# Four early pairs of q and k staged in the tile of w_in's sums, in a fused attention and feed-forward kernel, with every engine's order written anew

## The chip, the core and the metric

The kernel runs on one core of a Trainium2 chip. The metric is the device time of one execution in microseconds: three runs of the kernel before gave 353.08 as their median (352.15 to 353.31). The profile is a fourth execution; its own time was 353.37 us, and the span that its trace covers, from the first instruction to the last, is 351.6 us.

The engines are named as the profile names them: PE is TensorE (PEld its weight loads), DVE is VectorE, ACT is ScalarE, POOL is GpSimd and SP is SyncE. A `q` behind a name, as in SPq, is that engine's queue of DMA issues.

## The reference

Eight batches of eight-head attention with a bias that depends on the distance of two positions, then a feed-forward layer with a squared ReLU on all 4608 rows:

```python
scores = scale * np.matmul(q, k.transpose(0, 1, 3, 2))      # q, k, v: (8, 8, 576, 64)
scores = scores + bias.transpose(2, 0, 1)[None, :, :, :]    # bias_table[bucket(|i - j|)]
attn = softmax(scores)                                       # over the keys
x = np.matmul(attn, v).transpose(0, 2, 1, 3).reshape(4608, 512)
h = np.maximum(x @ w_in, 0.0)                                # w_in: (512, 2048)
out = (h * h) @ w_out                                        # w_out: (2048, 512)
```

Inputs and output are float32. The kernel computes in float16 with float32 sums.

## The kernel before

**Tiling.** Two heads make a pair, four pairs a batch, so there are 32 pairs, numbered from 0. A pair's q and k are loaded in natural layout into staging tiles (`qs`, `ks`, float16, 128x768), turned so that the head's 64 dimensions lie on partitions (`qt`, `kt`), and multiplied to scores in PSUM (line 954; the last 64 keys at line 1021 or 1149 through `kz`, which holds the two heads' keys on its diagonal; the last 64 queries at line 961). ScalarE takes the exponential into `pt` and `pm` (lines 976, 1006, 1030, 1136, 1159), VectorE multiplies by the exponential of the bias, kept in `tb_sb` (line 800), TensorE multiplies by v with a column of constants beside it that gives the row sums (`va` holds 4 tiles of 128 keys, `vm` the last 64 keys; lines 826 and 833, later 876 and 892), and VectorE divides by the row sums into `x`. x is turned into `xt`, and 512 rows at a time (a group, nine of them) go through the feed-forward layer. The first layer is line 1551 for group 0, plain, and line 1486 for the others, with seven products of sub-blocks in place of eight; the second layer is line 1331, with seven as well.

**Sums of weights.** The seven products need sums and differences of blocks of w_in. They lie in the tile `sw` (128 partitions, four parts of three blocks of 512 float16, so each part is 1536 wide); VectorE makes them in `late_sums` (line 1408), before group 1. Until then `sw` holds nothing.

**Staging.** There are three pairs of staging tiles, `qs`/`ks` 68/69, 70/71 and 72/73, handed out in turn to all 32 pairs by the ring `r_stg`. The load of pair p waits until pair p-3 has been turned. Pair 0 comes by two hardware queues in float32 (k from ACTq, q from SPq) into the tile `g` and is cast into its staging tile by ScalarE (line 650). Pairs 1 to 31, v of batches 0 and 1, and the weights are loaded by POOL with a cast on the way (line 428); at most eight of POOL's loads are under way at once (eight lanes, each with its own semaphore). In batches 0 and 1, TensorE turns q and k (line 1089) and VectorE or ScalarE copies them out of PSUM (lines 786 and 788); from batch 2 on, SP turns them by DMA.

**Batch 0 in halves.** For pairs 0 to 3 the queries are worked in two parts (256 and 320), so that group 0's first half can start after the first part of all four pairs: scores of three exponential steps per pair, then the values, then the transposition of x (line 1209), then group 0's first layer (line 1551).

**What sets the order.** Each step of the work is an operation with a number. The table `TURNS` gives for each engine the numbers in the order in which that engine is to issue them. `Plan.schedule` walks the five lists with a cost for every operation, to lay the five streams into one program and to choose buffers where a ring has several free. An engine issues strictly in its list's order, and waits at the head of its list for operands and buffers.

Of the kernel before, what the change touches and what calls it, by code (L numbers as in the profile page):

```python
# [40 lines left out]
LATE, T_STG = 7, 8  # L41
V_AFTER = 8
# [8 lines left out]
def _bucket(n):  # L51
# [42 lines left out]
""",  # L94
    "ACT": """
# [16 lines left out]
""",  # L112
    "DVE": """
# [214 lines left out]
def mm(n):  # L328
    return n / 2.4 + 2.5
# [6 lines left out]
def dve(n, rate=1.0, fix=160.0):  # L336
    return fix + n / (0.96 * rate)
# [1307 lines left out]
```

## Time and profile before

| | before |
|---|---|
| median of 3 runs | 353.08 us (352.15 to 353.31) |
| the profiled execution | 353.37 us |
| its span | 351.6 us |
| PE busy | 341.0 us, 97% |
| DVE busy | 311.4 us, 89% |
| ACT busy | 264.5 us, 75% |
| POOL busy | 164.4 us, 47% |

A busy PE is not PE at its peak: the ends of matmuls are modelled, and a stretch can be full of matmuls that run slowly. PEclk is the granted clock of TensorE (1.00 is full). The table by stretches gives each engine's busy time in a stretch, with the number of instructions in brackets. In the timeline a row is a run of like instructions: the start in us, the busy time in us, engine and line, the tile written and the tile read, their number, and in brackets the idle time of that engine just before the row and what ended it.

### The profile page before, as it was taken

The numbers are of one execution on the slowest core, as the hardware profiler recorded it, in microseconds if no ns is written. First come the engines' busy times: TensorE is split into PE (matmuls) and PEld (weight loads), VectorE is DVE, ScalarE is ACT, GpSimd is POOL, SyncE is SP. The second block draws the span as 40 slices with busy tenths as digits, with TensorE's granted clock in tenths as the row PEclk, the third lists the DMA queues.
The fourth block names the chain that finished last, engine by engine and source line by source line (L and its number), as shares of the span: only waits on it lengthen the run. The fifth ranks groups of instructions, "written<-read, shape, count | busy, mean of one in ns | idle before, by whom it ended". The sixth has DMA issues, their size and how long they took to land.

```text
span 351.6 us, 11335 instructions
## 1 busy us (share of the span) xinstructions
PE 341.0 (97%) x4672; PEld 278.0 (79%) x4672; DVE 311.4 (89%) x615; ACT 264.5 (75%) x370; POOL 164.4 (47%) x287
## 2 busy tenths in 40 slices
PE   8599999899999999999999999999999999999996
PEld 7378777777877887778877887787768988888885
DVE  4869999999998999799989998879998996899983
ACT  4879998499998689889978587869797952288300
POOL 6929587859787369684683495245100000000000
PEclk9989999999999999999999999999999999999999
DMA  9999999999999999999999999699622031200023
GB/s 164 134 201 185 187 152 164 177 135 137 133 158 175 218 134 135 152 191 162 164 69 161 185 113 157 130 162 122 88 69 81 2 59 54 67 32 3 30 84 126
DMA packets 161379, 44.39 MB, mean 126 GB/s; under 512 B 144688, under 2 KB 161328, under 8 KB 161328
## 3 DMA queue, kind: packets, MB, share of 16 engines
q0 software_dynamic: 74144, 14.53, 49.9%
q1 hardware_dynamic: 86928, 28.86, 45.9%
q8 instruction: 36, 0.59, 0.7%
q10 hardware_dynamic: 256, 0.30, 0.3%
q14 instruction: 15, 0.12, 0.1%
HBM read 36.94 MB, written 9.44 MB: 132 GB/s over the span
## 4 chain that ended last, share of the span: by engine, by line
PE 79%; DVE 9%; DMA 5%; ACT 4%; issue 1%; POOL 1%; SPq 0%; DVEq 0%; POOLq 0%
PE bank L1331 29%; PE bank L1486 25%; PE bank L892 8%; PE bank L954 7%; DVE g L1512 2%; DMA va<-in_v_dram 2%; DMA qt<-qs 2%; PE bank L833 2%; DVE pt L800 2%; ACT pt L1136 2%; PE bank L1551 2%; PE bank L1149 1%; DVE s L1290 1%; PE bank L961 1%; DVE g L447 1%; DVE x L915 1%
## 5 line engine op out<-in xcount | busy, mean ns | idle before, releaser
L1136 ACT ACTIVATE pt<-bank 128x1024 f16<-128x1024 f32 x112 | 110.2, 1035 | 14.5 <-PE bank L954 13.8
L428 POOL DMA_DIRECT2D qs<-in_q_dram x79 | 55.8, 710 | 28.8 <-DMA qt<-qs 17.4
L428 POOL DMA_DIRECT2D ks<-in_k_dram x79 | 55.6, 712 | 21.8 <-DMA kt<-ks 12.1
L800 DVE TENSOR_TENSOR pt<-pt,tb_sb 128x512 f16<-128x512 f16 (+3 forms) x108 | 61.1, 589 | 2.8 <-ACT pt L1136 1.7
L1331 PEld LDWEIGHTS <-g 128*128 128x128 f16 x576 | 54.5, 98 | 9.4 <-issue 2.2
L1512 DVE CUSTOM_DVE_ANT_0 g<-bank,y 128x512 f16<-128x512 f32 x88 | 58.5, 682 | 1.9 <-PE bank L1486 0.5
L1486 PEld LDWEIGHTS <-w_in_sb 128*128 128x128 f16 x576 | 50.3, 98 | 8.0 <-issue 2.7
L1331 PEld LDWEIGHTS <-s 128*128 128x128 f16 x432 | 41.0, 98 | 8.8 <-issue 3.1
L1518 ACT ACTIVATE y<-bank 128x512 f32<-128x512 f32 x68 | 39.5, 605 | 9.9 <-PE bank L1486 9.2
L954 PE MATMUL bank<-qt,kt 64*128 64x512 f16 (+1 forms) x288 | 41.6, 359 | 0.1
L1486 PEld LDWEIGHTS <-sw 128*128 128x128 f16 x416 | 37.4, 98 | 5.4 <-issue 1.4
L892 PE MATMUL bank<-va,pt 128*128 128x65 f16 x1120 | 40.2, 193 | 0.5 <-DVE pt L800 0.5
L892 PEld LDWEIGHTS <-pt 128*128 128x128 f16 x1120 | 37.1, 97 | 3.3 <-issue 1.6
L1331 PE MATMUL bank<-w_out_sb,g 128*128 128x256 f16 x288 | 36.3, 273 | 0.0
L1486 PE MATMUL bank<-xt,w_in_sb 128*128 128x256 f16 (+3 forms) x320 | 36.2, 251 | 0.0
L1331 PE MATMUL bank<-wt,g 128*128 128x256 f16 x288 | 36.1, 273 | 0.0
L1331 PE MATMUL bank<-w_out_sb,s 128*128 128x256 f16 x288 | 36.0, 273 | 0.0
L445 ACT ACTIVATE g<-g 128x1024 f16<-128x1024 f16 x33 | 34.9, 1070 | 0.5 <-DVE g L1512 0.4
L1486 PE MATMUL bank<-tx,sw 128*128 128x256 f16 x224 | 32.5, 273 | 0.0
L1486 PE MATMUL bank<-tx,w_in_sb 128*128 128x256 f16 x224 | 32.0, 273 | 0.0
L1366 ACT ACTIVATE y<-bank 128x512 f32<-128x512 f32 x19 | 11.3, 597 | 27.4 <-PE bank L1331 26.9
L1116 POOL COPY kz<-kt 64x64 f16<-64x64 f16 x62 | 18.7, 305 | 25.1 <-PE bank L1331 7.7
(103 smaller groups left out, 540.8 us busy)
## 6 DMA issues: line engine op xcount, KB each, us to landing
out_dram<-y SPq DMA_DIRECT2D x34, 256.0 KB, 2.7
f<-in_v_dram SPq DMA_DIRECT2D x24, 256.0 KB, 5.0
qs<-in_q_dram POOLq DMA_DIRECT2D x48, 64.0 KB, 3.9
ks<-in_k_dram POOLq DMA_DIRECT2D x48, 64.0 KB, 4.7
w_in_sb<-in_moe_w_in_dram POOLq DMA_DIRECT2D x4, 512.0 KB, 8.2
w_out_sb<-in_moe_w_out_dram POOLq DMA_DIRECT2D x4, 512.0 KB, 9.2
va<-in_v_dram POOLq DMA_DIRECT2D x8, 128.0 KB, 7.5
ks<-in_k_dram POOLq DMA_DIRECT2D x7, 144.0 KB, 5.2
```

The source lines that it names most:

```text
L428: lambda: io(eng.dma_start(out=out_(), in_=in_())),
L445: io(nc.scalar.activation(out=a(), in_=a(), func=SQUAREF))
L800: io(nc.vector.tensor_tensor(out=a, in0=a, in1=t, op=MULT))
L892: nc.tensor.matmul(of_head(st, e)[:, ts(i, 65)], pt[:, c : c + 128], va[:, jt, 2 * hp + e, 0:65], start=False, stop=(jt == 3), skip_group_ ...
L954: nc.tensor.matmul(banks[i][e], kt[rw[e], ts(jt, 128)], qt[rw[e], ds(q0, n)], start=True, stop=True)
L1116: io(eng.tensor_copy(out=dst[qb.slot][rw, rw], in_=src[qb.slot][rw, 512:576]))
L1136: nc.scalar.activation(out=p5(pts[pb.slot])[:, jt, :, 0:512], in_=in_two(st), func=EXPF, scale=SCALE)
L1331: nc.tensor.matmul(g_ps[bf.slot][:, ts(s_, HALF)], left(c, s_), right(c), start=(c == 0 and (s_ == 0 or apart) and i not in before), stop= ...
L1366: io(nc.scalar.activation(out=dst, in_=ps, func=COPYF, scale=OSC))
L1486: nc.tensor.matmul(ps()[:, ds(HALF * f + a, z - a)], left()[:, kk, ts(f, 128)], right(a, z)[:, kk, :], start=(first_ and f == 0 and a == 0 ...
L1512: nc.vector._custom_dve(dve_ops.TENSOR_ADD_SAT, out=dst, in0=src, in1=at(plus).rearrange("p (f s) -> p f s", f=2), s0=MOST, s1=0.0,)
L1518: io(nc.scalar.activation(out=dst, in_=src, func=RELUF if where else COPYF))
```

## The change

Six things are different.

- Pairs 3 to 6 are staged in `sw` (one part each, 768 columns for q and 768 for k) instead of the ring of three. The ring is left to pairs 0, 1, 2 and 7 to 31.
- The sums of w_in wait until the pair that was staged in their part has been turned.
- The five lists of `TURNS` are written anew. No operation is added or left out; some change the engine that does them (copies out of PSUM and squares between VectorE and ScalarE, copies into `kz` between POOL and VectorE).
- In POOL's list the first loads are those of q and k of pairs 1 to 3; v comes behind them.
- The planner that lays out the program counts POOL's casts and copies, and those operations of VectorE that read two SBUF tiles in 16 bits, as excluding each other (`Shared`, `PORT`).
- The arithmetic, the tile sizes and the queue by which each load comes are the same.

The diff, without the lines of `TURNS`:

```diff
+ROOMS = range(3, 7)
...
+class Shared(float):
+    pass
...
+PORT = 130.0
...
-        mode = None
+        mode, port = None, {"DVE": (0.0, 0.0), "POOL": (0.0, 0.0)}
...
-            took = op.engs[e]
+            took, held = op.engs[e], at
+            if isinstance(took, Shared):
+                a, z = port["POOL" if e == "DVE" else "DVE"]
+                if a < at < z - PORT:
+                    took, held = took + z - at - PORT, z
+                port[e] = held, at + took
...
 def dve(n, rate=1.0, fix=160.0):
-    return fix + n / (0.96 * rate)
+    t = fix + n / (0.96 * rate)
+    return Shared(t) if rate > 1.0 and fix == 160.0 else t
...
-    b_stg = [Buf(r_stg) for _ in range(4 * B)]
+    b_stg = [Buf(Ring(1) if p in ROOMS else r_stg) for p in range(4 * B)]
+
+    def staged(p, w):
+        if p in ROOMS:
+            return sw_sb[:, p - ROOMS[0]].rearrange("p a k c -> p (a k c)")[:, ts(w, 12 * D)]
+        return stg[b_stg[p].slot][w]
+
+    turned_out = {}
...
-                lambda: six(stg[b_stg[p].slot][w]),
+                lambda: six(staged(p, w)),
...
-                t = stg[b_stg[p].slot][w]
+                t = staged(p, w)
...
             o = P.add({"PE": 12 * 25.0 if b < SIX else 5 * mm(128)}, tr, l_qk[p, w] + [l_id], [bank, b_stg[p], qb], T - 3000, after, "c" if b < SIX else "f")
+            turned_out.setdefault(p, []).append(o)
...
-                late["ops", u] = late_sums(512, s_, terms, l_win + plain[4 + u], due + 10.0 * u)
+                late["ops", u] = late_sums(512, s_, terms, l_win + plain[4 + u] + turned_out[ROOMS[u]], due + 10.0 * u)
```

Two places of the new lists, with the old ones. The first is POOL at the start, from its third load on. `qs`/`ks` 70/71 hold pair 1, 72/73 pair 2, 68/69 pair 0 and then pair 3 in the kernel before; `sw` holds pairs 3 and 4 in the changed one. Before:

```order
L428 DMA qs_72<-in_q_dram 96x2x384
L428 DMA qs_70<-in_q_dram 96x2x384
L428 DMA va<-in_v_dram 128x8x64
L428 DMA ks_73<-in_k_dram 96x2x384
L428 DMA vm<-in_v_dram 64x4x64
L428 DMA va<-in_v_dram 128x8x64
L428 DMA qs_68<-in_q_dram 96x2x384
L1116 COPY kz<-kt_78 64x64 x2
L428 DMA ks_69<-in_k_dram 96x2x384
L428 DMA va<-in_v_dram 128x8x64
L1116 COPY kz<-kt_79 64x64
L428 DMA va<-in_v_dram 128x8x64
```

Changed:

```order
L440 DMA qs_72<-in_q_dram 96x2x384
L440 DMA ks_71<-in_k_dram 96x2x384
L440 DMA sw<-in_k_dram 96x2x384
L440 DMA va<-in_v_dram 128x8x64
L440 DMA vm<-in_v_dram 64x4x64 x2
L440 DMA va<-in_v_dram 128x8x64 x2
L1136 COPY kz<-kt_78 64x64
L440 DMA sw<-in_q_dram 96x2x384
L1136 COPY kz<-kt_80 64x64
L440 DMA va<-in_v_dram 128x8x64
L440 DMA sw<-in_q_dram 96x2x384
L1136 COPY kz<-kt_79 64x64
```

The first `vm` load, which stood at POOL's head before, has moved behind the loads of q and k; one copy into `kz` for pair 0 has gone to VectorE; pair 3's k comes before all of v; the fourth tile of v (the last row of the one, the third row from the end of the other) is POOL's twelfth load in both, behind three copies into `kz` before and two now.

The second place is ACT at the start, from its first cast to the exponentials of pair 3's first part. Before:

```order
L650 ACTIVATE ks_69<-g_97 96x768
L650 ACTIVATE qs_68<-g_97 96x768
L786 ACTIVATE kt_78<-bank 128x576
L536 ACTIVATE tb_sb<-bank 128x8x64
L786 ACTIVATE qt_75<-bank 128x576
L1006 ACTIVATE pt<-bank 128x2x2x256 x2
L1030 ACTIVATE pm<-bank 128x256 x2
L1006 ACTIVATE pt<-bank 128x2x2x256 x4
L1030 ACTIVATE pm<-bank 128x256
L1006 ACTIVATE pt<-bank 128x2x2x256 x2
L1030 ACTIVATE pm<-bank 128x256
```

Changed:

```order
L669 ACTIVATE qs_68<-g_97 96x768
L555 ACTIVATE tb_sb<-bank 128x8x64
L805 ACTIVATE qt_74<-bank 128x576
L555 ACTIVATE tb_sb<-bank 128x8x64
L805 ACTIVATE kt_80<-bank 128x576
L1025 ACTIVATE pt<-bank 128x2x2x256 x2
L1049 ACTIVATE pm<-bank 128x256
L1025 ACTIVATE pt<-bank 128x2x2x256 x3
L1049 ACTIVATE pm<-bank 128x256 x2
L1025 ACTIVATE pt<-bank 128x2x2x256 x3
L1049 ACTIVATE pm<-bank 128x256
```

The cast of pair 0's k has gone to VectorE, and a second copy of the bias table has come in its place; three copies of q and k have become two. The exponentials are the same eight long and four short ones.

More of the change, by code (lines that the diff above doesn't have):

```diff
@@ L629, in load_rows @@
             (
-                lambda e=e: rows(stg[b_stg[p].slot][w])[:, 0:4, ds(64 * e, D)],
+                lambda e=e: rows(staged(p, w))[:, 0:4, ds(64 * e, D)],
                 src[e, 0:512, :].rearrange("(t p) d -> p t d", p=128), (512, 14.5),
@@ L635, in load_rows @@
             (
-                lambda: stg[b_stg[p].slot][w][0:64, 512:640].rearrange("p (e d) -> p e d", e=2),
+                lambda: staged(p, w)[0:64, 512:640].rearrange("p (e d) -> p e d", e=2),
                 src[:, 512:S, :].rearrange("e p d -> p e d"), (128, 14.5),
@@ L718, in load_v_fp32 @@
                 o = P.add(
-                    {"POOL": ns},
+                    {"POOL": Shared(ns)},
                     lambda room=room, dst=dst: io(nc.gpsimd.tensor_copy(out=dst(), in_=room())),
@@ L1072, in pair @@
                         nc.sync.dma_start_transpose(
-                            out=dst[qb.slot].rearrange("p (t d) -> p t d", d=128), in_=stg[b_stg[p].slot][w][:, 0:640]
+                            out=dst[qb.slot].rearrange("p (t d) -> p t d", d=128), in_=staged(p, w)[:, 0:640]
                         )
@@ L1116, in sp @@
                     io(eng.tensor_copy(out=dst[qb.slot][rw, rw], in_=src[qb.slot][rw, 512:576]))
-                spread.append(one_of({"DVE": 205.0, "POOL": 320.0} if b < DT_QK else {"POOL": 320.0}, sp, [evac[w]] + z_fix[min(p, 1)], [qb], T - 1000))
+                spread.append(one_of({"DVE": 205.0, "POOL": Shared(320.0)} if b < DT_QK else {"POOL": Shared(320.0)}, sp, [evac[w]] + z_fix[min(p, 1)], [qb], T - 1000))
         if b < HALVES:
```

172 rows, old and new, of the table TURNS are left out of this document.

## Prediction

> **What bounds the kernel now.** I read the page's first two parts, then busy time by stretches, then the waits at the start, then the timeline of the first 27 us engine by engine. The first two rows are from the page, the others from the table by stretches (busy us of PE, PEld, DVE, ACT and POOL, then the granted clock, the share of the DMA engines and GB/s):
>
> ```profile
> span 351.6 us, 11335 instructions
> PE 341.0 (97%) x4672; PEld 278.0 (79%) x4672; DVE 311.4 (89%) x615; ACT 264.5 (75%) x370; POOL 164.4 (47%) x287
> ...
> 0.00:25.80 25.80, 19.89 (x387) 15.84 (x388) 16.59 (x52) 17.55 (x26) 15.90 (x30) 0.93 1.23 165
> 25.80:52.00 26.20, 26.20 (x404) 21.09 (x403) 25.40 (x63) 26.05 (x38) 20.47 (x39) 1.00 1.50 176
> 52.00:100.00 48.00, 47.09 (x704) 37.16 (x703) 46.85 (x96) 41.41 (x59) 36.91 (x61) 1.00 1.32 150
> 100.00:150.00 50.00, 50.00 (x666) 38.90 (x663) 44.85 (x84) 42.37 (x58) 34.52 (x58) 1.00 1.42 160
> 150.00:200.00 50.00, 49.70 (x738) 40.20 (x737) 45.70 (x89) 40.79 (x56) 29.51 (x48) 1.00 1.23 156
> 200.00:250.00 50.00, 49.81 (x650) 40.28 (x648) 45.10 (x80) 40.71 (x60) 26.08 (x50) 1.00 1.02 135
> 250.00:300.00 50.00, 49.88 (x697) 41.43 (x695) 44.98 (x88) 33.54 (x45) 1.04 (x5) 1.00 0.28 60
> 300.00:351.60 51.60, 48.41 (x444) 43.11 (x441) 41.90 (x71) 22.04 (x35) 0.00 (x0) 1.00 0.16 54
> ```
>
> From 25.8 us, where the first feed-forward layer begins, to 300 us TensorE is idle for 1.5 us in all (0.91 of it between 52 and 100). It does the same matmuls in either kernel, so after 25.8 us there is next to nothing to win. The end comes earlier only if the work ahead of 25.8 us is over earlier, and only if the 25.8 to 300 us stay as full. In the start TensorE is idle for 5.9 of 25.8 us. The waits and TensorE's and ScalarE's timelines there:
>
> ```profile
> PE bank L833 <- DMA va<-in_v_dram: 2.4, 1, 2.4
> ACT pt L1006 <- PE bank L954: 2.1, 2, 1.9
> POOL qs L428 <- PE bank L1089: 6.4, 1, 6.4
> ...
> 18.02 0.31 PE L833 MATMUL bank<-va,pt 128*128 128x65 f16 x5 [2.35 <-DMA va<-in_v_dram]
> 18.56 0.61 PE L954 MATMUL bank<-qt,kt 64*128 64x256 f16 x8
> 24.17 0.61 PE L1209 MATMUL bank<-id_sb,x 128*128 128x128 f16 x8
> ...
> 6.47 0.84 ACT L650 ACTIVATE qs<-g 96x768 f16<-96x768 f32 x1
> 8.90 0.60 ACT L536 ACTIVATE tb_sb<-bank 128x512 f16<-128x512 f32 x1 [0.36 <-PE bank L524]
> 9.59 0.65 ACT L786 ACTIVATE qt<-bank 128x576 f16<-128x576 f16 x1
> 10.16 1.94 ACT L1006 ACTIVATE pt<-bank 128x1024 f16<-128x1024 f32 x2
> 16.71 0.39 ACT L1030 ACTIVATE pm<-bank 128x256 f16<-128x256 f32 x1
> 19.00 1.94 ACT L1006 ACTIVATE pt<-bank 128x1024 f16<-128x1024 f32 x2 [1.90 <-PE bank L954]
> ```
>
> From 10.16 to 17.10 us ScalarE works without a break on the exponentials of pairs 0 to 2: it sets the pace. Then it idles for 1.90 us. It waits for pair 3's scores (18.56), these stand in TensorE's list behind the values of pair 0, and those wait for the fourth tile of v. Here the start loses about 2 us on its bounding engine, and x's transposition at 24.17 and the feed-forward layer at 25.80 follow from it. The clock falls as well:
>
> ```profile
> 12.00:16.00 4.00, 2.52 (x46) 1.57 (x46) 3.46 (x9) 3.71 (x7) 3.54 (x8) 1.00 1.40 112
> 16.00:20.00 4.00, 1.98 (x35) 1.64 (x34) 1.75 (x8) 2.10 (x4) 3.42 (x5) 0.90 1.27 179
> 20.00:24.00 4.00, 4.00 (x68) 2.92 (x66) 2.46 (x9) 3.13 (x7) 0.00 (x0) 0.68 1.26 203
> ```
>
> In the 4 us after the stall the granted clock is 0.68, TensorE has no idle time left, and ScalarE idles for 0.87 us.
>
> **The change part by part.** The rows are POOL's loads, and for single loads the time from issue to landing in us (last column):
>
> ```profile
> 1.46 0.76 POOL L428 DMA_DIRECT2D vm<-in_v_dram  x1 [1.00 <-DVE g L489]
> 8.91 0.65 POOL L428 DMA_DIRECT2D qs<-in_q_dram  x1 [1.72 <-PE bank L524]
> 11.75 0.89 POOL L428 DMA_DIRECT2D va<-in_v_dram  x1
> 25.85 0.63 POOL L428 DMA_DIRECT2D qs<-in_q_dram  x1 [6.43 <-PE bank L1089]
> ...
> g<-in_q_dram SPq DMA_DIRECT2D x1, 288.0 KB, 4.8
> qs<-in_q_dram POOLq DMA_DIRECT2D x1, 144.0 KB, 3.9
> va<-in_v_dram POOLq DMA_DIRECT2D x1, 128.0 KB, 6.2
> ```
>
> The three rows at the foot are pair 0's q, issued at 1.6 us, pair 3's q at 8.91, and the fourth tile of v at 11.75, which landed at 18.0.
>
> *Fourth tile of v.* It stays POOL's twelfth load. Before, pair 3's q had to wait for pair 0 to be turned (8.91), and the tile for one more copy into `kz`. Now pair 3 has its own room, and the last thing ahead of the tile is a copy that needs pair 2's k, which ScalarE copies out right before its first exponential. The corresponding row of before ends at 10.24, so I put the issue at about 10.5, 1.2 us earlier. Taking 6.2 us again it lands at 16.7; taking the 3.9 us of the load at 8.91, at 14.4, and then ScalarE has no gap at all. So the gain lies between 1.2 and 1.9 us; I take 1.5. The 6.43 us that POOL stood still before 25.85 go too, but no wait of TensorE or ScalarE on those loads shows, so they count nothing.
>
> *First exponentials.* ScalarE's list now begins with the cast of q, which could start at 6.47, and has 0.84 + 0.60 + 0.65 + 0.60 + 0.65 = 3.34 us ahead of the first exponential: 9.8 against 10.16, a gain of 0.35. Against it: POOL no longer waits for VectorE's fills, so its loads start up to 1.0 us earlier, and five loads of q and k run beside pair 0's q on the same DMA engines. By the two POOL rows a load in a crowd takes up to 2.3 us longer (6.2 against 3.9); by the 4.8 of pair 0's q, which already ran beside others, the loss may be nothing. Bounds 0.35 gained to 1.95 lost; I take 0, nearer the 4.8, which is this very load. The Trainium skill, DMA: Bandwidth & Descriptors, section SWDGE vs HWDGE vs iDMA, says that each DMA engine serves the two kinds of queues in turn; by that rule pair 0's q must give way, and this speaks against the new order of the loads; how much, only a run can show.
>
> *Clock.* Without the stall TensorE need not fall to half speed behind it. The gain is between 0 and ScalarE's 0.87 us of idle there; I take 0.5, since the stretches before (2.52 busy of 4) stay as thin. The Trainium skill, TensorE: Matmul & The Clock Gate, section What's actually happening, lets the clock fall after an idle window of about 3.4 us. The trace disagrees: a pause of 2.35 us in a stretch that was half busy was enough. By the page the changed kernel would keep its clock, and this term would be the whole 0.87.
>
> *VectorE's share.* I compared which engine has each operation in the two orders. Of those that ran between 25.8 and 100 us, 13 come from ScalarE to VectorE (four copies of q or k, six evacuations, two squares, one copy of x) and 11 go the other way, and it gets three small ones from POOL and gives one back. With these durations, columns count, total busy time and mean ns:
>
> ```profile
> L788 DVE COPY kt<-bank 128x576 f16<-128x576 f16 x5 | 3.7, 749 | 0.5 <-PE bank L1089 0.5
> L1567 DVE TENSOR_SCALAR g<-bank 128x512 f16<-128x512 f32 x6 | 4.1, 686 | 0.1
> L447 DVE TENSOR_TENSOR g<-g 128x1024 f16<-128x1024 f16 x39 | 26.1, 687 | 0.5 <-ACT g L1565 0.3
> L788 DVE COPY xt<-bank 128x512 f16<-128x512 f16 x7 | 2.7, 416 | 0.2 <-PE bank L1209 0.2
> L1116 DVE COPY kz<-kt 64x64 f16<-64x64 f16 x2 | 0.5, 264 | 0.0
> ```
>
> that is 4 x 0.75 + 8 x 0.69 + 0.4 = 8.9 us in, and two copies of q or k, six evacuations, one square and one and a half copies of x out, 7.0; with some 0.5 for the small ones (a copy into `kz` of 0.26 and two fills that are no longer) VectorE has 2.4 us more. In those 74.2 us it is idle for 1.95. So what no longer fits is 0.5 us; bounds are 0 (if the rest of its work is shorter, below) and 2.4 (if its idle time is waiting that stays). I take 0.5 lost.
>
> *Casts apart from VectorE.* Two groups of one shape, 128x512 from two SBUF operands, differ in the mean: `sw` from w_in 477 ns against 410 where the second operand is `sw` itself.
>
> ```profile
> L1408 DVE TENSOR_TENSOR sw<-w_in_sb 128x512 f16<-128x512 f16 x8 | 3.7, 477 | 0.0
> L1408 DVE TENSOR_TENSOR sw<-w_in_sb,sw 128x512 f16<-128x512 f16 x4 | 1.6, 410 | 0.0
> ```
>
> If such stretching goes, VectorE and POOL gain some, but only what TensorE idles for can come out: 0.9 us between 52 and 100, nothing elsewhere. I count 0, bound 0.9.
>
> *Sums of w_in behind the turning of pairs 3 to 6.*
>
> ```profile
> L1408 DVE TENSOR_TENSOR sw<-w_in_sb x5: 409/414/819, 52.1 to 70.9; 128x512 f16<-128x512 f16 x5
> ```
>
> The first sum into `sw` runs at 52.1 us, some 17 us behind the last turning of q and k of batch 1: nothing.
>
> *The rest of the orders.* From 100 to 300 us there is 0.6 us to win; new orders may leave gaps, of which the stretch from 52 to 100 (0.9) is the worst that before shows. I count 0, bounds 0.6 gained and 1.8 lost.
>
> The sum: 1.5 + 0 + 0.5 - 0.5 = 1.5 us less. The profiled execution took 353.37, 0.29 above the median of the runs; 353.37 - 1.5 = 351.9 there, and **351.6 us** as a median.
>
> **The rivals.** *Pair 0's q lands late (slower).* Everything in the start hangs on that load, and it is the one that the new first loads run beside. If it takes the 2.3 us more, the first exponential is at 12.1, the 6.94 us of the first three pairs end at 19.05, and pair 3 starts no earlier than before: the gain is gone. The pause is now ahead of the first scores; if the half clock follows from it, as it did at 16 to 20, it costs its 0.9 anew, and with VectorE's 0.5 the median is 354.5. It decides from 1.9 us of delay on, a landing more than 6.7 us after the issue. For it speaks the crowd of loads; against it that the 4.8 us already contain some of it.
>
> *The fourth tile of v still lands near 18.* Eleven loads with the same bytes are ahead of it in both kernels. If the DMA engines and not POOL's issue were the limit, the stall stays, and with VectorE's 0.5 it is 353.6. Against it: POOL's loads at 8.91 took 3.9 us, so the engines had caught up by then.
>
> *VectorE becomes the bound between 26 and 100 us.* The whole 2.4 are lost behind a gain of 2.0: 353.5. For it speaks 72.25 us busy of 74.2; against it that it also starts earlier.
>
> *All of it works.* No gap on ScalarE (1.9), the clock stays (0.9), VectorE fits and the 0.5 us of its waits for POOL go: 3.3 less, 349.8. (By the page on the clock gate the second of these four is certain; by the trace it is not.)
>
> **How the numbers follow.** The forecast gets 0.40, the late q 0.20, the late tile 0.12, VectorE as the bound 0.12, all of it 0.16. About 0.3%, 1.06 us, is what a measurement of this kernel can tell from no change. Faster, below 352.0: 0.34 of the forecast's 0.40, 0.16, and 0.03 of the middle cases: 0.53. Slower, above 354.1: 0.15 of the late q's 0.20 and 0.05 of the others: 0.20. Within: 0.27. The forecast's own range is 350.6 to 352.6; to leave out no more than 2 in 10 it must reach to both sides, 349.6 to 354.4.
>
> **What would show it.** Right: no idle time of ScalarE near 1.9 us before pair 3's exponentials, which start before 18; the first matmuls of line 1551's counterpart near 23.8 to 24.5 instead of 25.8; a granted clock of 1.00 in the 20 to 24 us row; TensorE busy for at least 47 of 48 us between 52 and 100. Wrong: the cast of pair 0's q later than 7.2 us; TensorE waiting for v again for over 1 us; or TensorE idle for over 2 us between 26 and 300, with VectorE as what it waits for.

## The result, and the profile after

The changed kernel takes **352.47 us** as the median of 20 runs (350.82 to 353.19), the kernel before 354.79 us beside it (20 runs, 352.15 to 357.72): a ratio of **0.9935, interval 0.9916 to 0.9954**. A second measurement gave 0.999 (0.9956 to 1.0024; 352.87 against 353.32 us). So the first is clear of 1 and the second is not; the gain is somewhere between nothing and 0.8%. The predicted range, 349.6 to 354.4 us, holds the time; the kernel before stood 1.7 us above the 353.08 from which the forecast was worked out. Medians count all runs; the ratios leave out runs over 1.5% longer than the fastest of the same kernel. The profiled execution took 352.39 us (span 350.3) against 353.37 (351.6). By stretches, with the columns as in the prediction:

```profile
12.00:16.00 4.00, 2.66 (x42) 1.73 (x38) 3.92 (x11) 4.00 (x6) 3.86 (x6) 0.88 1.52 172
16.00:20.00 4.00, 4.00 (x66) 3.00 (x64) 3.06 (x11) 2.78 (x6) 2.36 (x5) 0.69 1.23 194
20.00:24.00 4.00, 3.88 (x67) 2.47 (x66) 3.93 (x13) 3.91 (x8) 1.06 (x2) 1.00 1.36 200
25.80:52.00 26.20, 24.94 (x410) 19.98 (x405) 24.15 (x60) 24.14 (x36) 18.50 (x34) 1.00 1.41 165
52.00:100.00 48.00, 47.19 (x676) 36.81 (x674) 47.24 (x95) 40.16 (x58) 41.60 (x61) 1.00 1.54 152
100.00:300.00 200.00, 199.77 (x2741) 161.89 (x2738) 181.59 (x335) 156.57 (x218) 92.47 (x156) 1.00 1.04 127
```

And rows of its timelines (PE, then ACT, then POOL):

```profile
14.51 0.45 PE L1108 MATMUL bank<-id_sb,sw 96*64 96x96 f16 x12 [0.97 <-DMA sw<-in_q_dram]
23.78 0.39 PE L1571 MATMUL bank<-xt,w_in_sb 128*128 128x256 f16 x2
35.26 0.28 PE L852 MATMUL bank<-va,pt 128*128 128x65 f16 x4 [1.26 <-issue]
...
9.54 1.96 ACT L1025 ACTIVATE pt<-bank 128x1024 f16<-128x1024 f32 x2
16.81 1.94 ACT L1025 ACTIVATE pt<-bank 128x1024 f16<-128x1024 f32 x2 [0.81 <-PE bank L973]
...
10.12 0.90 POOL L440 DMA_DIRECT2D va<-in_v_dram  x1
```

The fourth tile of v is issued at 10.12 us (11.75 before), and TensorE no longer waits for it. In its place TensorE waits 0.97 us for pair 3's q, which the new list loads as the eleventh of twelve. Pair 3's exponentials start at 16.81 instead of 19.00, the feed-forward layer (line 1571, 1551 before) at 23.78 instead of 25.80. The clock still falls, only 4 us earlier: full from 4.80 to 15.04, half to 18.46 (before: half from 19.17 to 22.58). Between 25.8 and 52 us, where TensorE was full before, it now idles 1.26 us in the midst of a group of values, on no operand ("issue"); below this is called the hole. From the layer's first matmul to the last matmul of all it is 323.0 us (322.3 before). So 2.0 us are won in the start, and 0.7 are lost behind it; some 0.3 us of both is only a shift, since the new list has four more matmuls of scores ahead of the layer (391 matmuls in all against 387).

### The profile page after: what moved, and what is told of

Its sections match the earlier page's. It is cut to its first block, busy times and chain, and to the rows that moved or that the text cites. A ratio compares the mean times of both kernels' runs of the same rounds, so it can differ in the third digit from the quotient of the medians.

```text
span 350.3 us, 11312 instructions
## 1 busy us (share of the span) xinstructions
PE 341.2 (97%) x4672; PEld 277.6 (79%) x4672; DVE 314.8 (90%) x618; ACT 261.0 (75%) x370; POOL 170.7 (49%) x283
## 4 chain that ended last, share of the span: by engine, by line
PE 77%; DVE 13%; ACT 3%; DMA 3%; issue 3%; SPq 0%; POOL 0%; DVEq 0%; ACTq 0%; POOLq 0%
PE bank L1351 28%; PE bank L1506 25%; PE bank L911 8%; PE bank L973 7%; DVE pt L819 2%; PE bank L1169 2%; DMA sw<-in_q_dram 1%; DMA g<-in_q_dram 1%; PE bank L852 1%; PE bank L980 1%; PE bank L1571 1%; ACT pt L1156 1%; PE bank L895 1%; DVE g L1532 1%; DVE s L1310 1%
## 5 line engine op out<-in xcount | busy, mean ns | idle before, releaser
L819 DVE TENSOR_TENSOR pt<-pt,tb_sb 128x640 f16<-128x640 f16 (+3 forms) x108 | 60.2, 577 | 1.9 <-ACT pt L1156 1.6
L440 POOL DMA_DIRECT2D ks<-in_k_dram x75 | 52.8, 708 | 17.4 <-DMA kt<-ks 11.9
L440 POOL DMA_DIRECT2D qs<-in_q_dram x75 | 53.0, 711 | 16.3 <-DMA kt<-ks 10.3
L1538 ACT ACTIVATE y<-bank 128x512 f32<-128x512 f32 x69 | 39.9, 607 | 21.0 <-PE bank L1506 17.2
L1506 PE MATMUL bank<-xt,w_in_sb 128*128 128x256 f16 (+3 forms) x320 | 37.1, 251 | 0.0
L457 ACT ACTIVATE g<-g 128x1024 f16<-128x1024 f16 x30 | 31.4, 1064 | 4.4 <-DVE g L1532 4.3
L1506 PE MATMUL bank<-tx,w_in_sb 128*128 128x256 f16 x224 | 32.8, 273 | 0.0
L459 DVE TENSOR_TENSOR g<-g 128x1024 f16<-128x1024 f16 x42 | 29.1, 715 | 0.3
L1386 ACT ACTIVATE y<-bank 128x512 f32<-128x512 f32 x22 | 13.1, 597 | 21.3 <-PE bank L1351 19.3
```

The source lines that it names most:

```text
L440: lambda: io(eng.dma_start(out=out_(), in_=in_())),
L457: io(nc.scalar.activation(out=a(), in_=a(), func=SQUAREF))
L459: io(nc.vector.tensor_tensor(out=a(), in0=a(), in1=a(), op=MULT))
L819: io(nc.vector.tensor_tensor(out=a, in0=a, in1=t, op=MULT))
L1386: io(nc.scalar.activation(out=dst, in_=ps, func=COPYF, scale=OSC))
L1506: nc.tensor.matmul(ps()[:, ds(HALF * f + a, z - a)], left()[:, kk, ts(f, 128)], right(a, z)[:, kk, :], start=(first_ and f == 0 and a == 0 ...
```

## The experiments

Twelve runs. "The start" below is the time of the layer's first matmul, "the tail" the time from there to the last matmul. The number with an interval is the ratio to the kernel before, run on the same chip beside it; the median behind it is the run's own. A room is the place of one of the pairs 3 to 6 in `sw`.

**Both kernels once more.** No edit.

> The changed kernel once more, unaltered. Theory A (the hole of 1.3 us at 33.8 us belongs to the program: it comes where a fetch of instructions meets a burst of weight loads): a second profile shows the same hole at the same place, TensorE's busy time between 25.8 and 52 us is again 24.9 to 25.0 us, the first matmul of the feed-forward layer starts at 23.8 us, the profiled execution takes 352.4. Theory B (the hole is an accident of one execution): it is absent or elsewhere, and the execution is about 1.3 us shorter, 351.1. Ratio to the kernel before by either: 0.9915 to 0.9955.

Measured: 0.999 (0.9956 to 1.0024), median 352.87 us; start 24.59, tail 322.8. The second profile of the changed kernel, ACT and then PE:

```profile
7.34 0.84 ACT L669 ACTIVATE qs<-g 96x768 f16<-96x768 f32 x1 [3.57 <-DMA g<-in_q_dram]
10.61 1.94 ACT L1025 ACTIVATE pt<-bank 128x1024 f16<-128x1024 f32 x2
...
14.71 0.45 PE L1108 MATMUL bank<-id_sb,sw 96*64 96x96 f16 x12
15.62 0.22 PE L845 MATMUL bank<-vm,pm 128*128 128x130 f16 x1 [0.47 <-ACT pt L1025]
16.13 0.77 PE L852 MATMUL bank<-va,pt 128*128 128x65 f16 x8 [0.29 <-DVE pt L819]
24.59 1.05 PE L1571 MATMUL bank<-xt,w_in_sb 128*128 128x256 f16 x8
35.56 0.28 PE L852 MATMUL bank<-va,pt 128*128 128x65 f16 x4 [0.76 <-issue]
```

Pair 0's q landed at 7.32 us instead of 6.58, the first exponentials are 1.1 us later and the layer 0.8. Here TensorE does not wait for pair 3's q (it landed at 14.20): in that wait's place it stands 0.47 us for ScalarE and 0.29 for VectorE, and the clock falls all the same, from 15.90 to 19.32. So the wait for pair 3's q belongs to the first profile and not to every execution. The hole is there again, in front of the same matmul (the 606th of 4672), smaller (0.76 us). Theory A holds for its place, not for its size.

> The kernel before once more, unaltered. Theory A (the first profile caught a fourth tile of v that was held up by accident: 6.2 us from issue to landing, with a fetch of 16 KB of TensorE's instructions that took 2.3 us beside it): a second profile shows the tile 4.2 to 4.7 us after its issue, at 15.8 to 16.4 us, TensorE waits under 1 us for it, and the feed-forward layer starts at 23.4 to 24.5 us. Theory B (the late tile belongs to the kernel, as the prediction took it): it lands at 17.5 or later, TensorE waits over 2 us, the layer starts at 25.5 or later. The ratio is 1.000 within its interval by either.

Measured: 0.9983 (0.9944 to 1.0022), median 353.93. The profiled execution was a long one (355.67 us) and stands here for its start alone. Its PE timeline, and the row of instruction fetches among the DMA queues between 14 and 18 us (count, MB, share of 16 engines' time):

```profile
19.35 0.43 PE L833 MATMUL bank<-va,pt 128*128 128x65 f16 x5 [3.49 <-DMA va<-in_v_dram]
27.02 1.16 PE L1551 MATMUL bank<-xt,w_in_sb 128*128 128x256 f16 x9
```

```profile
q8 instruction: 1, 0.02, 5.0%
```

One fetch of 16 KB of instructions (TensorE's, as the last section infers) took 5.0% of 16 x 4 us, 3.2 us; the tile, issued at 11.95, landed 1.6 us after the fetch's end, 7.36 us after its issue. In the first profile that row reads 3.6% (2.3 us), and the tile again landed 1.6 us after the fetch's end. Theory B holds in this profile as in the first: the tile is late, and it is still under way when the fetch comes, at 14.1 and 14.6 us. That the fetch holds up the tile is inferred from the two landings; that both are slow for a third reason is not excluded. Nor need the tile be late in every execution: single runs of this kernel go down to 349.62 us.

**The rooms alone.**

```diff
 (kernel before, lists of TURNS unaltered)
+ROOMS = range(3, 7)          # second run: range(3, 4)
+    b_stg = [Buf(Ring(1) if p in ROOMS else r_stg) for p in range(4 * B)]
...
```

> The kernel before with pairs 3 to 6 staged in the tile of w_in's sums, and all five lists as before. Theory A (the room alone lets the loads start earlier, the fourth tile of v is what TensorE waited for): pair 3's q is issued near 7 instead of 8.91 us, the fourth tile of v at 10.5 to 11 instead of 11.75; TensorE's wait for v falls from 2.35 to about 1.3 us, the feed-forward layer starts at 24.8 and the time is 1.0 us less than before, ratio 0.997. Theory B (the gain of the changed kernel comes from its lists, of loads above all): the wait for v stays over 2 us, the layer starts at 25.5 to 25.9, ratio 0.999 to 1.001.

Measured: **0.9916 (0.9886 to 0.9946)**, median **350.87 us**, 2.0 us under the changed kernel on the same chip. PE, POOL and ACT of its timeline, and two of its stretches:

```profile
7.09 0.45 PE L1097 MATMUL bank<-id_sb,ks 96*64 96x96 f16 x12
15.40 0.31 PE L841 MATMUL bank<-va,pt 128*128 128x65 f16 x5 [0.42 <-DMA va<-in_v_dram]
22.34 1.92 PE L1560 MATMUL bank<-xt,w_in_sb 128*128 128x256 f16 x16
...
7.14 0.68 POOL L429 DMA_DIRECT2D sw<-in_q_dram  x1
10.45 0.89 POOL L429 DMA_DIRECT2D va<-in_v_dram  x1
...
10.07 1.94 ACT L1014 ACTIVATE pt<-bank 128x1024 f16<-128x1024 f32 x2
16.74 1.96 ACT L1014 ACTIVATE pt<-bank 128x1024 f16<-128x1024 f32 x2
```

```profile
12.00:16.00 4.00, 2.84 (x56) 1.91 (x57) 3.41 (x9) 3.76 (x7) 2.62 (x7) 1.00 1.67 164
16.00:20.00 4.00, 3.63 (x80) 2.80 (x81) 3.60 (x15) 4.00 (x7) 3.47 (x6) 1.00 1.21 179
```

The old lists with the rooms do all that the changed kernel does and more: pair 3's q goes out at 7.14 us (9.30 in the changed kernel), the fourth tile at 10.45, landed at 15.35, the clock does not fall (no change is recorded, and turning takes 0.45 us from the first on, against 0.69 at half clock), pair 3's exponentials follow without a gap, and the start is at 22.34. That is more than theory A put on it (24.8): it is the start of the rival in which all of it works, and the lists of the change are not needed for it. The tail is 323.3 us.

> The kernel before with the room for pair 3 alone: pairs 4 to 6 stay in the ring. Theory A (pair 3's loads and the fourth tile of v behind them are all that the room gives): the layer starts at 22.2 to 22.6 us, as with all four rooms, and the time is within 0.3 us of that kernel, ratio 0.990 to 0.993. Theory B (the rooms of pairs 4 to 6 matter, since GpSimd stood still for 6.4 us at the load of pair 6): the start is the same, but TensorE loses 0.5 us or more between 25 and 52 us, ratio 0.994 or more.

Measured: 0.9948 (0.9919 to 0.9976), median 351.76; start 22.37, tail 323.8. A row of POOL's timeline, and one of the stretches:

```profile
22.35 0.63 POOL L429 DMA_DIRECT2D qs<-in_q_dram  x1 [3.32 <-PE bank L1097]
```

```profile
25.80:52.00 26.20, 26.20 (x441) 20.86 (x439) 25.59 (x63) 26.05 (x38) 20.56 (x39) 1.00 1.54 184
```

The start is the same to 0.03 us, so it comes from pair 3's room. POOL stands still for 3.32 us again, and TensorE is full from 25.8 to 52 us all the same: theory A for the trace. The runs (0.9 us longer, another chip) overlap with those of all four rooms, but the ratio lies where theory B put it; whether the other three rooms are worth something is open.

**The order of the first twelve loads.**

```diff
 POOL of the kernel with the rooms, loads only (49/51 q, k of pair 1; 61/63 of pair 2; 69/71 of pair 3)
-67 51 61 49 57 63 65 53 69 71 55 59
+49 63 61 51 71 57 65 67 55 53 69 59
```

> The kernel before with the room, and the first twelve loads of GpSimd in the order of the changed kernel (q and k of pairs 1 to 3 ahead of v); the other lists as before. The fourth tile of v is the twelfth load, behind two copies into kz of pair 0 and one of pair 1. Theory A (the order of loads is what counts, the other engines' lists are worth little): the layer starts at 23.8 to 24.5 us and the time is 1.5 to 2.0 us less than before, ratio 0.994 to 0.996. Theory B (the loads only help if ScalarE and TensorE take their work in the new order too): the wait for v or for pair 3's q stays over 1.5 us, the layer starts at 25 us or later, ratio 0.998 to 1.000.

Measured: 1.0072 (1.0046 to 1.0098), median 356.31, though the start was at 23.28 us. The tail was 328.7 us. TensorE's longest waits (us in total, times, longest), and a stretch:

```profile
PE bank L1160 <- POOL kz L1127: 1.9, 1, 1.9
PE bank L1099 <- DMA sw<-in_q_dram: 1.7, 1, 1.7
PE bank L964 <- ACT pt L1147: 1.4, 1, 1.4
PE bank L886 <- DVE g L1531: 1.3, 1, 1.3
```

```profile
150.00:200.00 50.00, 48.11 (x724) 38.73 (x723) 43.12 (x84) 40.20 (x55) 27.56 (x46) 1.00 1.23 145
```

Neither theory had long waits between 50 and 200 us. The planner walks the lists with costs, and with another order of loads it gave 557 of 2434 operations other buffers, banks of PSUM above all. So the run was repeated with the buffers held:

```diff
+    told = P.schedule(...)    # with the old order
+    for i, x in zip(places, loads):
+        told[i] = by[x]       # only the twelve loads change places
```

> The kernel with the rooms and the old lists, and GpSimd's first twelve loads in the order of the changed kernel; other than in the earlier run of that order, the planner has laid out the program and chosen its buffers (banks of PSUM and others) with the old order, and only the places of the loads are swapped behind it. Theory A (the earlier run lost its 5 us behind the start because the planner's buffers came out otherwise for 557 of 2434 operations): the layer starts at 22.5 to 23.3 us and the time is within 1 us of the kernel with the rooms alone, ratio 0.991 to 0.996. Theory B (the order of the loads itself does the harm): ratio 1.004 or more.

Measured: 0.9983 (0.9955 to 1.0011), median 352.25, start 23.61, tail 323.5. The 5 us behind the start are gone, as theory A said; but the start, the time and the ratio lie outside its ranges, and so does the ratio for theory B. PE and ACT of its timeline and a stretch:

```profile
14.44 0.70 PE L1097 MATMUL bank<-id_sb,sw 96*64 96x96 f16 x24 [1.10 <-DMA sw<-in_q_dram]
23.61 1.92 PE L1560 MATMUL bank<-xt,w_in_sb 128*128 128x256 f16 x16
...
10.70 1.94 ACT L1014 ACTIVATE pt<-bank 128x1024 f16<-128x1024 f32 x2
17.79 1.94 ACT L1014 ACTIVATE pt<-bank 128x1024 f16<-128x1024 f32 x2
```

```profile
16.00:20.00 4.00, 4.00 (x67) 3.16 (x67) 3.28 (x13) 3.93 (x6) 3.59 (x6) 0.65 1.20 171
```

This is like the first profile of the changed kernel: the wait for pair 3's q, the clock at half from 15.40 to 18.81, the layer 1.3 us later than with the old order of loads. But half of that is there before the wait: pair 0's q landed at 7.09 us instead of 6.55, and ScalarE's first exponentials start 0.6 us later (10.70 against 10.07), pair 3's 1.05 later, again without a gap just ahead of them. The other four lists are the old ones here. So the new order of the loads gives back 1.3 of the 3.5 us that the rooms win at the start in these profiles, about half of it through pair 0's q; the rest comes with the wait for pair 3's q and the half clock, which the run does not separate. By the runs it is 1.4 us (medians 350.87 and 352.25, on two chips; the intervals of the ratios do not overlap).

> The changed kernel with GpSimd's first twelve loads in the order of the kernel before (vm and a tile of v early, k of pair 3 tenth); all else as changed. TensorE's new list asks for pair 3's k at 10.1 us, between the scores of pair 0; as the tenth load it lands near 13.5. Theory A (loads and lists belong together): TensorE stands 3 us at the turning of that k, the feed-forward layer starts after 26 us, ratio 1.000 to 1.004. Theory B (lists are what gained, the order of the loads is of little weight): the wait is under 1 us, the layer starts by 24.5 us, ratio 0.993 to 0.996.

(The changed kernel, the same twelve loads swapped the other way; buffers not held.) Measured: 1.0076 (1.0049 to 1.0104), median 356.50, start 26.84. A row of PE's timeline, and two stretches:

```profile
10.99 0.69 PE L1110 MATMUL bank<-id_sb,ks 96*64 96x96 f16 x12 [0.93 <-DMA ks<-in_k_dram]
```

```profile
8.00:12.00 4.00, 2.64 (x60) 2.25 (x56) 2.67 (x7) 1.63 (x4) 2.04 (x4) 0.50 1.74 172
12.00:16.00 4.00, 4.00 (x60) 2.15 (x57) 2.59 (x5) 3.33 (x5) 3.55 (x7) 0.50 1.25 99
```

The start is as late as theory A said, but not by one wait of 3 us: short waits and a clock at half from 7.85 to 18.09. With 765 operations in other buffers the run tells nothing of the lists alone, and no run has the new lists of the other engines with the old loads and the buffers held.

**Idle matmuls against the clock.** Matmuls of zeros, 128x128, whose result is overwritten at once, in the waits:

```diff
+    def idles(n, out):
+        for _ in range(n):
+            io(nc.tensor.matmul(out, idle_sb, idle_sb, start=True, stop=True))
+            idles(34, ...)   # before: ahead of the values of pair 0
+            idles(14, ...)   # changed kernel: ahead of the turning of pair 3's q
+            idles(4 / 6 / 6) # rooms alone: pair 3's q, its k, the values of pair 0
```

> The kernel before with 34 matmuls of zeros ahead of the values of pair 0, in the 2.35 us in which TensorE waited for the fourth tile of v; the tile lands as late as before. Theory A (half of what a late tile costs is the clock that falls behind it): the granted clock does not fall behind the wait, the feed-forward layer starts near 24.3 us instead of 25.8, and the time is 1.5 to 1.9 us under the kernel before, ratio 0.995 to 0.996. Theory B (the wait itself is the cost, the clock 0.5 us as the prediction put it): ratio 0.998 to 0.999.

Measured: 0.9992 (0.9961 to 1.0023), median 353.05; start 23.38, tail 324.0. PE's timeline, then the fetches among the DMA queues between 14 and 18 us, then a stretch:

```profile
14.77 2.06 PE L499 MATMUL bank<-g 128*128 128x128 f16 x34
23.38 0.83 PE L1557 MATMUL bank<-xt,w_in_sb 128*128 128x256 f16 x6
```

```profile
q8 instruction: 1, 0.02, 1.9%
```

```profile
200.00:250.00 50.00, 48.47 (x633) 38.56 (x633) 44.63 (x79) 40.40 (x59) 28.17 (x50) 1.00 1.10 134
```

The clock held, and the start came 2.4 us earlier. But the run can't price the clock: the fetch took only 1.2 us this time (1.9%) and the tile landed at 15.79 us, 4.6 after its issue, so the wait went too. Of the 2.4 us only 0.8 reached the last matmul; TensorE idles 1.5 us between 200 and 250 us.

> The changed kernel with 14 matmuls of zeros (128x128, overwritten at once) ahead of the turning of pair 3's q, in the 0.97 us that TensorE waited there. Theory A (the half clock of 3.41 us behind that wait withheld up to 1.7 us, and it came because TensorE was idle): the clock stays at 1.00 from 10 to 30 us, the feed-forward layer starts at 22.4 to 22.9 us instead of 23.8 to 24.6, and the time is 351.0 to 351.6, that is 1 to 1.5 us under the changed kernel. Theory B (TensorE was waiting for others there anyway, the half clock is worth under 0.5 us): the layer starts at 23.3 or later, 352.3. For the hole at 33.8 us: 28 more instructions lie ahead of it; if it hangs on the place in TensorE's stream where instructions are fetched, it moves to an earlier operation or changes in length; if it hangs on the operation, it stays in the values of the same pair.

Measured: 0.9964 (0.9933 to 0.9994), median 353.17, its runs in two groups (four from 350.45 to 351.03, one at 352.15, seven from 353.17 to 354.09). The profile is of the upper group; a row of ACT's and one of PE's timeline, and two stretches:

```profile
7.90 0.84 ACT L673 ACTIVATE qs<-g 96x768 f16<-96x768 f32 x1 [4.10 <-DMA g<-in_q_dram]
39.74 1.05 PE L1577 MATMUL bank<-xt,w_in_sb 128*128 128x256 f16 x8 [1.65 <-DMA w_in_sb<-in_moe_w_in_dram]
```

```profile
8.00:12.00 4.00, 3.21 (x80) 2.38 (x80) 2.48 (x7) 3.73 (x6) 3.42 (x6) 0.72 1.90 155
12.00:16.00 4.00, 4.00 (x50) 1.92 (x46) 3.45 (x10) 3.21 (x5) 4.00 (x8) 0.50 1.49 146
```

Pair 0's q landed 6.26 us after its issue. TensorE waited 1.9 us before the first scores, the clock fell at 9.76 for 6.8 us, and the start was at 25.46. Nothing is decided on the clock behind pair 3's q, since the idle matmuls stood behind the wait that mattered. The 1.65 us at 38 us are a wait for w_in. The hole in the values of the same pair is gone.

> The kernel before with all four rooms (its lists as before) and 16 matmuls of zeros in TensorE's three short waits: 4 and 6 ahead of the turning of pair 3's q and k, 6 ahead of the values of pair 0. Theory A (the clock is at stake in every execution, and falls in some): the clock never falls at the start, the spread of the runs narrows, and the mean is 0.3 to 0.5 us under the kernel with the rooms alone, ratio to the kernel before 0.989 to 0.991. Theory B (with these loads the start is busy enough): no difference, or 0.1 us more, ratio 0.991 to 0.993.

Measured: 0.9934 (0.9904 to 0.9964), median 351.01, start 22.05, tail 323.3. The clock does not fall in its profile, as without the idle matmuls, and the spread did not narrow (349.57 to 354.67, against 349.68 to 351.71): theory B.

**Pair 3's q earlier in the changed kernel.**

```diff
 twelve loads of POOL, buffers held
-49 63 61 51 71 57 65 67 55 53 69 59
+49 63 61 51 71 69 57 65 67 55 53 59     # second run: 67 (vm) ahead of all
```

> The changed kernel, its buffers unaltered, with the load of pair 3's q moved ahead of all of v (sixth load instead of eleventh); v's first tiles go out 0.65 us later, its fourth no later. Theory A (what the changed kernel lacked at the start was pair 3's q, landed at 14.5): TensorE no longer waits 0.97 us for it, the clock does not fall in most executions, the feed-forward layer starts at 22.3 to 22.9 us and the time is 1 to 1.5 us under the changed kernel, ratio to the kernel before 0.989 to 0.993. Theory B (the start waits for v's fourth tile right behind it, and the clock falls all the same): the layer starts at 23.5 or later, ratio 0.993 to 0.997.

Measured: 0.9948 (0.9915 to 0.9981), median 351.80, again two groups (six runs up to 351.31, six from 352.29). PE:

```profile
7.72 0.69 PE L1108 MATMUL bank<-id_sb,qs 96*64 96x96 f16 x12 [0.41 <-ACT qs L669]
16.16 0.69 PE L1108 MATMUL bank<-id_sb,sw 96*64 96x96 f16 x12
25.92 1.05 PE L1571 MATMUL bank<-xt,w_in_sb 128*128 128x256 f16 x8
35.85 0.68 PE L852 MATMUL bank<-va,pt 128*128 128x65 f16 x8
```

The wait for pair 3's q is gone, and yet this execution (353.56 us) starts the layer at 25.92: twelve turning matmuls take 0.69 us until 16 us, 0.45 in the changed kernel's first profile at 7.5. The clock came on at 21.21 only. With the same instructions in the same order the hole has shrunk to 0.12 us, in front of the same 606th matmul (eight matmuls take 0.68 us there). The upper group fits such executions, the lower one the start of theory A; with one profile that is not shown.

> As the run with pair 3's q moved, and the short load of v's last keys back at GpSimd's head, where the kernel before had it, so that the first long load beside pair 0's q goes out 0.77 us later. Theory A (with four long loads behind it pair 0's q lands late in some executions: 4.96, 5.70 and 6.26 us after its issue in three profiles of this order, 4.77 to 5.19 in five of the old order): it lands within 5.2 us, and the time is 0.5 to 1 us under the run with pair 3's q alone. Theory B (the landings differ by chance): no difference, within 0.3 us.

Measured: 1.0079 (1.0049 to 1.0109), median 356.65. The swap put that load ahead of the fill of its tile. So this kernel leaves out the last 64 rows of v of four heads, which the fill overwrites, and VectorE waits for the load before it may fill:

```profile
7.00 0.41 DVE L578 MEMSET vm<- 128x264 f32 x2 [5.70 <-DMA vm<-in_v_dram]
```

So the run measures that wait and says nothing on theory A or B.

## Why the prediction was right, step by step

**The sum.** -1.5 us was forecast; the two first profiles differ by 1.0 us, the medians by 2.3 and 0.5 us in the two measurements. The sum holds because errors of both signs met, and the time lies in the range although the kernel before was 1.7 us longer than the forecast took it: in part luck.

**Fourth tile of v: right.** Issue at 10.12 (10.5 forecast), landing at 15.10 (14.4 to 16.7), and 16.42 in the repeat; TensorE no longer waits for it. Pair 3's exponentials are 2.2 us earlier (19.00 to 16.81), in the second pair of profiles 2.8 (20.92 to 18.07): more than the 1.2 to 1.9 of the forecast. The bounds took the 6.2 us for a crowd; the two profiles of the kernel before, with 2.3 and 3.2 us of instruction fetch beside it, point to the fetch. What I had not asked was which load would be late next: pair 3's q stood just ahead of the tile in the new list. (ScalarE was not quite without a break from 10.16 to 17.10 us in the kernel before: it waited 0.19 us at 14.7, which changes no sum.)

**First exponentials: the size was off, both ways.** 0 was taken; they came 0.62 us earlier in one profile and 0.45 later in the next. Of the 1.06 us between the two, 0.74 is the landing of pair 0's q, and the rest goes with the clock, which was on from 4.80 us in the one and from 9.08 in the other, after the first turning (8.93 in the kernel before): a part that the prediction had no term for. Pair 0's q landed 4.92 to 6.26 us after its issue in six profiles with the new head of POOL's list (five long loads from 1.3 us on), and 4.77 to 5.26 in seven with the old head. The two ranges overlap, but with the buffers held the new order had the first exponentials 0.6 us later. So a part of the slower rival is in the measured time, though never the 6.7 us from which it decides. The cast of pair 0's q after 7.2 us, named as what would make the prediction wrong, occurs in the repeat (7.34).

**Clock kept, 0.5 gained: failed.** The sign named for it, 1.00 in the row from 20 to 24 us, came true, but only because the fall had moved ahead of that row. The clock fell in both profiles of the changed kernel, after windows of 3.41 us in which TensorE was busy for 2.08 and 2.46 us. By the Trainium skill, TensorE: Matmul & The Clock Gate, section What's actually happening, the fall comes after an idle window of about 3.4 us; the trace again disagrees, since these windows were more than half busy. In place of a gain stands what the rooms alone show: without the fall and without the wait for pair 3's q the layer starts at 22.34 instead of 23.6 to 24.6. The two were not separated. The single runs of the kernel before in three measurements (the 87 that the ratios use), sorted by their mean granted clock, give means of 351.9 us at 1.00 (8 runs), 353.1 at 0.995 (35) and 354.0 at 0.99 or less (44): about a microsecond for each window at half clock, if the clock is the cause and not the sign of a longer wait. The sorting is blurred, since an execution with a long stretch at half speed can read 1.00, as the one of 353.56 us does.

**VectorE, 0.5 lost: not seen.** Between 52 and 100 us TensorE is busy for 47.19 and 47.41 us (47.09 before), VectorE for 47.24. It has more work in all (busy 314.8 us against 311.4), but between 25.8 and 100 us it is busy for 71.39 and 71.95 us (72.25 before) and not for 2.4 more. VectorE did not become the bound.

**Rest of the orders, 0 (0.6 gained to 1.8 lost): the size was off, for a reason not named.** The loss of 0.7 us in the tail is smaller than the hole of 1.26 us. In both profiles it ends 1.3 to 1.5 us after the end of a fetch of 16 KB, which began when TensorE had 9 and 27 matmuls left to the hole. The other profiles with this kernel's instructions fall into line: with pair 3's q moved the fetch began 57 matmuls ahead, and 0.12 us were left of the hole; with the short load of v at the head as well it began 67 ahead, and there is none; in the two profiles of the kernel before it began 85 and 95 matmuls ahead of the 606th. So TensorE ran out of instructions there, as far as the traces can show it; what sets the start of the fetch was not tried.

**Only the start can be won: right.** Leaving out the run of the new loads without held buffers, thirteen executions with starts from 22.05 to 27.36 us have tails of 321.7 to 324.0. The time is the start plus 323 us, give or take one.

**A version that beats both** is the rooms with the old lists: 350.87 us, 0.9916 of the kernel before (0.9886 to 0.9946), against 352.87 us of the changed kernel on the same chip. With the new order of the loads alone beside the rooms it is 352.25, about the changed kernel's time; what the new lists of the other four engines are worth is not shown.

## What to carry to other kernels

When a late load is taken off the path, list the loads behind and beside it by landing time against use: the next late one takes over. Here pair 0's q and pair 3's q, both later in the new order, cost 1.3 of 3.5 us with the buffers held. A table of numbers that orders the work also feeds the planner that chooses buffers, so an experiment on the order has to hold the buffers (1.0072 against 0.9983 for the same twelve loads). Test the room apart from the new lists, and take more than one profile of each kernel where its runs spread over more than the effect.

## What the runs showed of the hardware

- The clock's windows of 3.41 us do not start with the kernel: the same program had its clock on at 4.80 us in one execution and at 9.08 in another, and one with TensorE's same instructions at 21.21; these times leave different remainders of 3.41 us, while the stretches between two changes are whole multiples of it (10.24, 3.41, 6.83). The Trainium skill, TensorE: Matmul & The Clock Gate, section What's actually happening, calls the window free-running; the traces agree.
- The granted-clock column says 1.00 ahead of the first change that was recorded: in the last-named execution it does so while turning takes 0.69 us in place of 0.45. Ahead of the first change, read the clock from the length of such matmuls.
- Instructions are fetched during the run: 36 times 16 KB (q8 of the changed kernel's page, 0.59 MB, 63 bytes for each of TensorE's 9344 matmuls and weight loads, from which it is inferred that they are TensorE's). One took 0.9 us at best and 3.2 us beside POOL's loads. Where one came late, TensorE stood still in the midst of a group (1.26 and 0.76 us); where one was slow (2.3 and 3.2 us), a load landed late, 1.6 us after its end.
